# Decoding 20 of 44 float64 weights with sign and low bits taken over by ScalarE

## The chip, the cores and the metric

The kernel runs on one core of a Trainium2 chip. The metric is the device time of one execution in microseconds. The engines that matter are TensorE (PE: matrix products into PSUM), VectorE (DVE), ScalarE (ACT), GpSimd (POOL) and the DMA queues that SyncE (SP) and ScalarE issue. Each engine runs its own instructions in order and waits for the others by semaphores.

## The reference

Three stages on 8 batches of 576 tokens, cut to what matters:

```python
# attention in chunks of 64 tokens, 8 heads of 64 (q, k, v float32)
scores = 0.125 * q_c @ k_c^T;  attn = softmax(scores);  x = attn @ v_c
# first block: weights in float64
h = maximum(x @ w_in, 0);  u, v = h[..., :512], h[..., 512:]
v_n = (v - mean(v)) / sqrt(var(v) + 1e-6)
x = (u * (w_spatial @ v_n + b_spatial)) @ w_out
# second block
u = x + ((x^T @ U) @ V)^T
out = u + maximum(u @ w_ch1, 0) @ w_ch2
```

`w_in` (512x1024), `w_out` (512x512), `w_ch1` (512x2048), `w_ch2` (2048x512), `U` and `V` arrive as float64. [...]

## The kernel before

**Numbers.** Every product is made of three f16 matmuls (`mm3`, L150 to 155): both sides are split into a high half and a low half, and high x high, high x low and low x high are added in PSUM. A tile of activations so is cast by ScalarE (high half) and subtracted by VectorE or GpSimd (low half) before TensorE can use it. `x`, `xd`, `hid`, `gt`, `tr` and `ph` are such tiles.

**Weights.** The 44 weight tiles of 128 x 512 are numbered: 0 to 3 `w_u` and 4 to 7 `w_v` (the halves of `w_in`), 8 to 11 `w_o` (`w_out`), 12 to 27 `w_1` (`w_ch1`), 28 to 43 `w_2` (`w_ch2`). Each goes through a decode:

- `dec_load` (L160): a DMA brings 128 x 512 integers of 64 bits, the low word first, either into one of three buffers `st` (tag `ld4`, shared with the loads of q and k) or, for 12 of the late ones, into a part of the final weight area `wch` that is still free.
- `dec_abs` (L166): ScalarE multiplies the high words, read as float32, by 2^-111 into a buffer `dt` (L176). Late weights have two buffers `dt` (tag `o`), earlier ones three (tag `hid`, which the hidden layer uses later).
- `dec_bits` (L179): VectorE shifts `dt` left by three (L183), ORs in the top three bits of the low word (L184) and the sign bit of the high word (L187).
- `dec_parts` (L191): ScalarE casts `dt` to the high f16 half (L194) and GpSimd subtracts for the low half (L195).

**Order.** The first five attention tiles run first (`gen_first`), then weights 4 to 7 and 0 to 3 are decoded, then the spatial weights, weights 8 to 11, U and V (`gen_dec`). After that `gen_moe` for batches 0 and 1 runs, mixed with the last four early attention tiles, and the late weights 12 to 43 are handed out in the order 12, 28, 13, 29, ... (`late`, L298): whenever a piece of matmuls is done and the due time of the next weight has come, `tick` calls `next_rest`, which decodes one weight and may first copy a single element of the tile just written (`gate`, L174), so that the decode is not taken up too early. From attention tile 9 on, three streams (`gen_attn`, `gen_moe`, `gen_ch`) are merged by `Flow`, a simulated clock with costs written by hand. `gen_ch` runs the second block in 9 slices of 512 tokens; before it uses hidden block f, `want(f)` makes sure that the late weights up to 2f + 2 have been handed out. All weights are decoded by about 250 us; from then on TensorE works through attention, first block and second block without them. The instructions of this order then pass through a scheduler that simulates the engines and orders each engine's queue by it, so a change of one operation can move others on every engine.

**Names at the two places that matter.** `xd` (L419 to 421) is the attention output of the fifth tile of a pair of batches, used by `gen_moe` as `pb<-w,xd`. `rz`, `bs`, `mv` are the normalisation of `gen_moe`. `mx`, `se`, `sp` are the softmax of an attention tile (`a_softmax`, `a_norm`, L386 to 400), `ph` its f16 halves (L552, L553), which a DMA transposes to `pt` (L555); `g` and `gt` (L678 to 683) are the gated product of `gen_moe`, `hid` the hidden layer of `gen_ch` (L822, L824), `tr` the output of the first block (L746), transposed by DMA at L752.

Of the kernel before, what the change touches and what calls it, by code (L numbers as in the profile page):

```python
# [8 lines left out]
F32 = mybir.dt.float32  # L9
F16 = mybir.dt.float16  # L10
U32 = mybir.dt.uint32
I64 = mybir.dt.int64
ACTF = mybir.ActivationFunctionType
ALU = mybir.AluOpType
# [88 lines left out]
def moe_kernel(  # L103
# [12 lines left out]
    nc = tc.nc  # L116
    NT = q.shape[0]

    const = ctx.enter_context(tc.tile_pool(name="const", bufs=1))
# [36 lines left out]


    stage = {}

    def dec_load(src, name, cols, st=None, eng=nc.sync):  # L160
        if st is None:
            st = sb.tile([128, 512], I64, tag="ld4", name="st", bufs=3)
        eng.dma_start(out=st[:, 0:cols], in_=src)
        stage[name] = (st, cols)

    def dec_abs(name, g=None):  # L166
        st, cols = stage[name]
        if isinstance(name, int) and name < 12:
            t = sb.tile([128, 2, 512], F16, tag="hid", name="dt", bufs=3)
            t = t.rearrange("p a n -> p (a n)").bitcast(F32)  # L170
        else:
            t = sb.tile([128, 512], F32, tag="o", name="dt", bufs=2)
        if g is not None:
            nc.scalar.copy(out=t[0:1, 0:1], in_=g[0:1, 0:1])  # L174
        hi = st[:, 0:cols].bitcast(U32)[:, 1::2]
        nc.scalar.activation(out=t[:, 0:cols], in_=hi.bitcast(F32), func=ACTF.Copy, scale=W_SC)  # L176
        stage[name] = (st, cols, t)

    def dec_bits(name):  # L179
        st, cols, t = stage[name]  # L180
        w = st[:, 0:cols].bitcast(U32)
        tb = t[:, 0:cols].bitcast(U32)
        nc.vector.tensor_scalar(out=tb, in0=tb, scalar1=3, scalar2=None, op0=ALU.logical_shift_left)  # L183
        nc.vector.scalar_tensor_tensor(  # L184
            out=tb, in0=w[:, 0::2], scalar=29, in1=tb, op0=ALU.logical_shift_right, op1=ALU.bitwise_or
        )
        nc.vector.scalar_tensor_tensor(  # L187
            out=tb, in0=w[:, 1::2], scalar=0x80000000, in1=tb, op0=ALU.bitwise_and, op1=ALU.bitwise_or
        )
# [33 lines left out]
    def spatial_weights():  # L223
        sc = float(2 ** 14)
        for i in range(5):
            st = sb.tile([128, 512], I64, tag="ld4", name="st", bufs=3)
            f = st.bitcast(F32)[:, 0:S]
# [13 lines left out]
            yield  # L241
        st = sb.tile([128, 512], I64, tag="ld4", name="st", bufs=3)
        f = st.bitcast(F32)[:, 0:S]
# [15 lines left out]
    def gen_dec(part):  # L259
# [17 lines left out]
        def run(names, loaded=False, step=1700.0):  # L277
            n = len(names)
            for i in range(-1, n + 2):
                if i + 1 < n and not loaded:  # L280
                    ld(names[i + 1])
                if 0 <= i < n:
                    dec_abs(names[i])
                if 0 <= i - 1 < n:
                    dec_bits(names[i - 1])
                    fin(names[i - 1])
                yield "wait", step
# [12 lines left out]

    wi = wch.rearrange("p f a k n -> p (f a k n)").bitcast(I64)

# [13 lines left out]
    def next_rest(g):  # L316
        i = given[1]
        load_rest(i + 1)
        n = late[i]
        dec_abs(n, g)  # L320
        if i == 11:
            load_rest(16, nc.sync)
        elif 12 <= i < 24:
            load_rest(min(i + 4, 24))
        dec_bits(n)
        dec_parts(n)
        given[1] += 1
# [99 lines left out]
    def first_loads():  # L427

        room = []
        for tag, n, bufs in (("uT", SLICE, 2), ("uT", SLICE, 2), ("gt", S, 1), ("u32", S, 1)):  # L430
            dt, sh = (F32, [128, 4, n]) if tag == "u32" else (F16, [128, 2, 4, n])
            t = sb.tile(sh, dt, tag=tag, name="room", bufs=bufs)
            t = t.rearrange("p k n -> p (k n)") if tag == "u32" else t.rearrange("p a k n -> p (a k n)")
            t = t.bitcast(I64)
            room += [t[:, 0:512], t[:, 512:1024]]
# [557 lines left out]
```

## Time and profile before

| | us |
|---|---|
| median of three runs | 1299.94 |
| their spread | 1298.25 to 1302.38 |
| the profiled execution, its own time | 1298.71 |
| its span in the trace | 1296.9 |

| engine | busy us | share of the span |
|---|---|---|
| PE (TensorE) | 1251.6 | 97% |
| DVE (VectorE) | 507.3 | 39% |
| ACT (ScalarE) | 500.2 | 39% |
| POOL (GpSimd) | 504.5 | 39% |

The averages hide two very different stretches, so the profile is read by stretch. A line of the trace names the line of the kernel, the engine, the operation, `out<-in` by the program's names, the shapes, and the time. Times in the timeline count from the start of the span; a bracket at a row's end gives how long the engine stood idle before it and what ended that. The granted clock of TensorE averaged 0.987 of its full speed over the run.

### The profile page before, as it was taken

How to read it: one execution, taken by the hardware profiler on the slowest of the kernel's cores; microseconds unless marked ns; L12 is line 12 of the kernel's file. 1: busy time of each engine (PE TensorE's matmuls, PEld its weight loads, DVE VectorE, ACT ScalarE, POOL GpSimd, SP SyncE). 2: the span in 40 equal slices, each digit the busy share in tenths (PEclk: the TensorE clock that was granted, in tenths of full speed). 3: DMA queues.
4: the chain of work that ended last, by engine and by line, in shares of the span. 5: the costliest groups of instructions: out<-in, count | busy, mean ns of one | idle time of the engine just before them, and what ended most of it. 6: DMA issues, size and time to landing. Idle time of an engine off the chain costs nothing.

```text
span 1296.9 us, 21079 instructions
## 1 busy us (share of the span) xinstructions
PE 1251.6 (97%) x8612; PEld 708.7 (55%) x8612; DVE 507.3 (39%) x934; ACT 500.2 (39%) x1024; POOL 504.5 (39%) x630
## 2 busy tenths in 40 slices
PE   7798997999999999999999999999999999999998
PEld 4476554445665466645665466545654565444443
DVE  7885777545333633242233513241114211221211
ACT  4655556445454444433354324332123212221110
POOL 4765767637455555524365515222112211020000
PEclk8799998999999999999999999999999999999999
DMA  9445335522233322420123101200011001000000
GB/s 344 154 129 137 120 115 134 123 83 53 66 78 65 90 58 50 93 67 5 34 73 71 50 1 26 45 33 5 1 28 42 1 1 28 26 17 1 33 1 33
DMA packets 95369, 81.46 MB, mean 63 GB/s; under 512 B 69668, under 2 KB 70308, under 8 KB 95272
## 3 DMA queue, kind: packets, MB, share of 16 engines
q1 hardware_dynamic: 94120, 75.92, 21.4%
q10 hardware_dynamic: 1152, 4.19, 1.0%
q8 instruction: 67, 1.10, 0.4%
q14 instruction: 30, 0.25, 0.1%
HBM read 53.62 MB, written 9.44 MB: 49 GB/s over the span
## 4 chain that ended last, share of the span: by engine, by line
PE 80%; DVE 7%; DMA 5%; POOL 4%; ACT 2%; issue 2%; SPq 0%; DVEq 0%; POOLq 0%; ACTq 0%
PE acc L151 9%; PE phid L151 9%; PE phid L155 9%; PE phid L154 9%; PE acc L155 9%; PE acc L154 9%; PE pb L151 7%; PE pb L155 7%; PE pb L154 7%; DVE dt L184 2%; DVE dt L187 2%; DMA wch<-in_q_dram 1%; DMA tr<-tr 1%; DVE dt L183 1%; POOL wch L195 1%
## 5 line engine op out<-in xcount | busy, mean ns | idle before, releaser
L824 DVE SCALAR_TENSOR_TENSOR hid<-phid,hid 128x512 f16<-128x512 f32 x144 | 99.2, 689 | 356.4 <-ACT hid L822 356.1
L151 PE MATMUL phid<-uT,wch 128*128 128x512 f16 x576 | 218.6, 379 | 1.1 <-DVE x L786 0.6
L154 PE MATMUL phid<-uT,wch 128*128 128x512 f16 x576 | 218.6, 379 | 0.0
L155 PE MATMUL phid<-uT,wch 128*128 128x512 f16 x576 | 218.4, 379 | 0.0
L154 PE MATMUL acc<-hid,wch 128*128 128x512 f16 x576 | 218.3, 379 | 0.0
L155 PE MATMUL acc<-hid,wch 128*128 128x512 f16 x576 | 218.3, 379 | 0.0
L151 PE MATMUL acc<-hid,wch 128*128 128x512 f16 x576 | 207.9, 379 | 2.2 <-ACT hid L822 2.2
L155 PEld LDWEIGHTS <-wch 128*128 128x128 f16 x1152 | 112.8, 98 | 131.4 <-issue 0.3
L151 PEld LDWEIGHTS <-wch 128*128 128x128 f16 x1152 | 112.7, 98 | 122.4 <-issue 6.5
L154 PEld LDWEIGHTS <-wch 128*128 128x128 f16 x1152 | 112.8, 98 | 117.8 <-issue 1.7
L822 ACT ACTIVATE hid<-phid 128x512 f16<-128x512 f32 x144 | 85.4, 594 | 179.7 <-PE phid L155 179.5
L683 POOL TENSOR_TENSOR gt<-g,gt 128x288 f16<-128x288 f32 x64 | 49.3, 772 | 151.7 <-ACT gt L681 151.4
L379 POOL TENSOR_TENSOR vbd<-vf,vbd 64x512 f16<-64x512 f32 x54 | 63.9, 1183 | 91.0 <-ACT vbd L378 83.7
L749 POOL TENSOR_TENSOR tr<-x,tr 128x64 f16<-128x64 f32 x64 | 48.1, 773 | 93.1 <-issue 52.1
L366 POOL TENSOR_TENSOR qbd<-qk,qbd 64x512 f16<-64x512 f32 x54 | 62.3, 1154 | 52.1 <-ACT qbd L365 48.3
L151 PE MATMUL pb<-sp_m,vn 128*128 128x288 f16 x256 | 73.2, 286 | 2.8 <-DVE hid L824 1.5
L154 PE MATMUL pb<-gt,w 128*128 128x288 f16 x256 | 73.7, 288 | 2.1 <-POOL gt L683 2.1
L151 PE MATMUL pb<-gt,w 128*128 128x288 f16 x256 | 73.5, 288 | 1.8 <-ACT tr L746 1.7
L151 PE MATMUL pb<-xT,w 128*128 128x288 f16 x256 | 73.5, 287 | 0.7 <-ACT up L659 0.7
L155 PE MATMUL pb<-gt,w 128*128 128x288 f16 x256 | 73.6, 288 | 0.0
L154 PE MATMUL pb<-xT,w 128*128 128x288 f16 x256 | 73.5, 287 | 0.0
L155 PE MATMUL pb<-xT,w 128*128 128x288 f16 x256 | 73.5, 287 | 0.0
(177 smaller groups left out, 2224.9 us busy)
## 6 DMA issues: line engine op xcount, KB each, us to landing
st<-in_wk_dram SPq DMA_DIRECT2D x24, 512.0 KB, 4.0
out_dram<-ot SPq DMA_DIRECT2D x32, 256.0 KB, 2.0
vf<-in_v_dram SPq DMA_DIRECT2D x27, 256.0 KB, 2.7
qk<-in_q_dram SPq DMA_DIRECT2D x27, 256.0 KB, 2.7
qk<-in_k_dram SPq DMA_DIRECT2D x27, 256.0 KB, 3.0
room<-in_wk_dram SPq DMA_DIRECT2D x8, 512.0 KB, 7.2
wch<-in_wk_dram ACTq DMA_DIRECT2D x8, 512.0 KB, 4.3
wch<-in_q_dram SPq DMA_DIRECT2D x9, 256.0 KB, 6.3
```

What stands on the lines that cost most here:

```text
L151: m = nc.tensor.matmul(out=o, lhsT=wh, rhs=xh, start=start, stop=False)
L154: nc.tensor.matmul(out=o, lhsT=wh, rhs=xl, start=False, stop=False)
L155: nc.tensor.matmul(out=o, lhsT=wl, rhs=xh, start=False, stop=stop)
L183: nc.vector.tensor_scalar(out=tb, in0=tb, scalar1=3, scalar2=None, op0=ALU.logical_shift_left)
L184: nc.vector.scalar_tensor_tensor(out=tb, in0=w[:, 0::2], scalar=29, in1=tb, op0=ALU.logical_shift_right, op1=ALU.bitwise_or)
L187: nc.vector.scalar_tensor_tensor(out=tb, in0=w[:, 1::2], scalar=0x80000000, in1=tb, op0=ALU.bitwise_and, op1=ALU.bitwise_or)
L366: nc.gpsimd.tensor_tensor(out=qbd[r, 1, :, c, :], in0=qv[r], in1=qbd[r, 0, :, c, :], op=ALU.subtract)
L379: nc.gpsimd.tensor_tensor(out=vbd[r, 1, :, :, c, :], in0=vf[r], in1=vbd[r, 0, :, :, c, :], op=ALU.subtract)
L683: nc.gpsimd.tensor_tensor(out=gt[:, 1, m, c], in0=g, in1=gt[:, 0, m, c], op=ALU.subtract)
L749: nc.gpsimd.tensor_tensor(out=th[:, o0:o0 + n], in0=x2[:, m, t0:t0 + n], in1=th[:, t0:t0 + n], op=ALU.subtract)
L822: nc.scalar.activation(out=hd[:, 0, :], in_=p, func=ACTF.Relu)
L824: nc.vector.scalar_tensor_tensor(out=hd[:, 1, :], in0=p, scalar=0.0, in1=hd[:, 0, :], op0=ALU.max, op1=ALU.subtract)
```

## The change

For the weights 8 to 27 (the four of `w_o` and the sixteen of `w_1`) ScalarE gets two more operations in `dec_abs`, and VectorE keeps one of three in `dec_bits`. The first new operation reads the upper 16 bits of each low word as a number, multiplies it by 2^-13 and adds a bias of 2^-14 - 0.5 from a small constant tile, so that rounding to an integer leaves its top three bits; it writes them into the lower 16 bits of the low word. The second multiplies the high word, read as float32, by 2^-60 and writes it as f16 into the upper 16 bits of the low word, where nothing but the sign is left. The low word then holds sign and low bits in place, and one operation of VectorE shifts `dt` and ORs the word in. The weights 28 to 43 (`w_2`), 0 to 7, U and V stay as they were; since `w_1` and `w_2` alternate, every other late weight is decoded in the new way.

```diff
@@ -156,6 +157,11 @@
     stage = {}
+    low_bias = const.tile([128, 1], F32, name="low_bias")
+    nc.vector.memset(low_bias, float(2.0 ** -14 - 0.5))
+
+    def by_scalar(name):
+        return isinstance(name, int) and (8 <= name < 28)
 
@@ -174,12 +180,22 @@
         hi = st[:, 0:cols].bitcast(U32)[:, 1::2]
         nc.scalar.activation(out=t[:, 0:cols], in_=hi.bitcast(F32), func=ACTF.Copy, scale=W_SC)
+        if by_scalar(name):
+            part = st.bitcast(U16)
+            nc.scalar.activation(
+                out=part[:, 0::4], in_=part[:, 1::4], func=ACTF.Relu, scale=float(2.0 ** -13), bias=low_bias)
+            nc.scalar.activation(
+                out=part.bitcast(F16)[:, 1::4], in_=hi.bitcast(F32), func=ACTF.Copy, scale=float(2.0 ** -60))
         stage[name] = (st, cols, t)
 
     def dec_bits(name):
         st, cols, t = stage[name]
         w = st[:, 0:cols].bitcast(U32)
         tb = t[:, 0:cols].bitcast(U32)
+        if by_scalar(name):
+            nc.vector.scalar_tensor_tensor(
+                out=tb, in0=tb, scalar=3, in1=w[:, 0::2], op0=ALU.logical_shift_left, op1=ALU.bitwise_or)
+            return
         nc.vector.tensor_scalar(out=tb, in0=tb, scalar1=3, scalar2=None, op0=ALU.logical_shift_left)
```

In the changed kernel the two new operations are L185 and L187, VectorE's single one is L196, and the lines behind stand 16 further down (L176 became L182, the three old operations L199, L200 and L203, L194 became L210, L420 and L421 became L436 and L437).

**Place 1: the first use of `xd`.** On VectorE before, the stretch from the last half of `xT` to `xd`; `dt` with its numbers are the buffers of weights 8 to 10, `st` their loaded words:

```order
L414 TENSOR_TENSOR xT_199<-of_352,xT_199 128x4x128
L187 SCALAR_TENSOR_TENSOR dt_543<-st_539,dt_543 128x512
L599 TENSOR_SCALAR rz_650<-rz_650,mv_654,y_657 128x512
L183 TENSOR_SCALAR dt_547<-dt_547 128x512
L184 SCALAR_TENSOR_TENSOR dt_547<-st_541,dt_547 128x512
L636 BN_STATS bs_682<-rz_680 128x6
L187 SCALAR_TENSOR_TENSOR dt_547<-st_541,dt_547 128x512
L638 BN_AGGR mv_684<-bs_682 128x2
L183 TENSOR_SCALAR dt_556<-dt_556 128x512
L640 TENSOR_SCALAR mv_684<-mv_684 128x1
L184 SCALAR_TENSOR_TENSOR dt_556<-st_545,dt_556 128x512
L421 TENSOR_TENSOR xd_422<-of_405,xd_422 128x512
```

The same stretch of VectorE in the changed kernel, with buffer numbers two higher:

```order
L430 TENSOR_TENSOR xT_201<-of_354,xT_201 128x4x128
L196 SCALAR_TENSOR_TENSOR dt_545<-dt_545,st_541 128x512
L615 TENSOR_SCALAR rz_652<-rz_652,mv_656,y_659 128x512
L652 BN_STATS bs_684<-rz_682 128x6
L654 BN_AGGR mv_686<-bs_684 128x2
L656 TENSOR_SCALAR mv_686<-mv_686 128x1
L196 SCALAR_TENSOR_TENSOR dt_551<-dt_551,st_543 128x512
L437 TENSOR_TENSOR xd_424<-of_407,xd_424 128x512
```

Two single operations stand where six operations of the decode stood. On ScalarE before, the rows that lead to its half of `xd`:

```order
L176 ACTIVATE dt_547<-st_541 128x512
L194 CAST w8_79<-dt_543 128x512
L633 ACTIVATE rz_680<-pb_667 128x512
L603 CAST vn_608<-rz_650 128x512
L176 ACTIVATE dt_556<-st_545 128x512
L420 CAST xd_422<-of_405 128x512
```

On ScalarE in the changed kernel, the same rows (one more L185 and one more L187, those of weight 8, stand a few rows further up):

```order
L182 ACTIVATE dt_551<-st_543 128x512
L185 ACTIVATE st_543<-st_543,low_bias_93 128x512
L210 CAST w8_79<-dt_545 128x512
L649 ACTIVATE rz_682<-pb_669 128x512
L619 CAST vn_610<-rz_652 128x512
L182 ACTIVATE dt_560<-st_549 128x512
L185 ACTIVATE st_549<-st_549,low_bias_93 128x512
L187 ACTIVATE st_543<-st_543 128x512
L436 CAST xd_424<-of_407 128x512
```

Three new operations have come in among the six, and the two of weight 8 above them. On TensorE the low half of `xd` (L155 before) is now first used four matmuls later: eight products `pb<-xT,w` stand between its first two uses of the high half and it, where four stood.

**Place 2: the softmax of attention tile 9.** On VectorE before, from the maximum (`mx`) to the normalisation (`se`); `dt_2188` is a weight of `w_2`:

```order
L388 TENSOR_REDUCE mx_2221<-sp_2196 128x8
L391 TENSOR_TENSOR se_2223<-sp_2196,mx_2221 128x512
L678 SCALAR_TENSOR_TENSOR g_2267<-pb_2252,up_1691 128x288
L824 SCALAR_TENSOR_TENSOR hid_2239<-phid_2162,hid_2239 128x512
L397 TENSOR_REDUCE sp_2196<-se_2223 128x8
L183 TENSOR_SCALAR dt_2188<-dt_2188 128x512
L398 TENSOR_SCALAR sp_2196<-sp_2196 128x8
L184 SCALAR_TENSOR_TENSOR dt_2188<-wch_70,dt_2188 128x512
L399 RECIPROCAL sp_2196<-sp_2196 128x8
L187 SCALAR_TENSOR_TENSOR dt_2188<-wch_70,dt_2188 128x512
L400 TENSOR_TENSOR se_2223<-se_2223,sp_2196 128x512
```

On VectorE in the changed kernel (`dt_2246` is the next weight, one of `w_1`):

```order
L404 TENSOR_REDUCE mx_2223<-sp_2198 128x8
L407 TENSOR_TENSOR se_2225<-sp_2198,mx_2223 128x512
L840 SCALAR_TENSOR_TENSOR hid_2241<-phid_2164,hid_2241 128x512
L413 TENSOR_REDUCE sp_2198<-se_2225 128x8
L694 SCALAR_TENSOR_TENSOR g_2269<-pb_2254,up_1693 128x288
L199 TENSOR_SCALAR dt_2190<-dt_2190 128x512
L414 TENSOR_SCALAR sp_2198<-sp_2198 128x8
L196 SCALAR_TENSOR_TENSOR dt_2246<-dt_2246,st_2244 128x512
L200 SCALAR_TENSOR_TENSOR dt_2190<-wch_70,dt_2190 128x512
L415 RECIPROCAL sp_2198<-sp_2198 128x8
L203 SCALAR_TENSOR_TENSOR dt_2190<-wch_70,dt_2190 128x512
L416 TENSOR_TENSOR se_2225<-se_2225,sp_2198 128x512
```

The single operation of the next weight has come in ahead of the reciprocal. On GpSimd before, from the gated product `gt` to the low half of `ph`:

```order
L683 TENSOR_TENSOR gt_1948<-g_2184,gt_1948 128x288
L366 TENSOR_TENSOR qbd_91<-qk_1686,qbd_91 64x8x64 x2
L369 TENSOR_TENSOR kd_2226<-qk_1686,kd_2226 128x512
L195 TENSOR_TENSOR wch_70<-dt_2123,wch_70 128x512
L683 TENSOR_TENSOR gt_1948<-g_2267,gt_1948 128x288
L195 TENSOR_TENSOR wch_70<-dt_2188,wch_70 128x512
L553 TENSOR_TENSOR ph_2275<-se_2223,ph_2275 128x512
```

On GpSimd in the changed kernel:

```order
L699 TENSOR_TENSOR gt_1950<-g_2186,gt_1950 128x288
L382 TENSOR_TENSOR qbd_91<-qk_1688,qbd_91 64x8x64 x2
L385 TENSOR_TENSOR kd_2228<-qk_1688,kd_2228 128x512
L699 TENSOR_TENSOR gt_1950<-g_2269,gt_1950 128x288
L211 TENSOR_TENSOR wch_70<-dt_2190,wch_70 128x512
L211 TENSOR_TENSOR wch_70<-dt_2246,wch_70 128x512
L569 TENSOR_TENSOR ph_2277<-se_2225,ph_2277 128x512
```

`gt` now follows the splits directly, and two weights instead of one stand before `ph`. On ScalarE, a second cast (L210) and one L185 of a later weight have come in ahead of the cast of `ph`. Two pairs of L185 and L187 on words loaded straight into `wch` stand far ahead of their own weight on ScalarE: one right behind the cast of weight 0, one in the middle of the late decode.

## Rows read from the trace of the kernel before

**Rows 1.** Busy us and instructions by stretch, then TensorE's granted clock, DMA share, GB/s:

```profile
core 0: us, PE busy (x) PEld busy (x) DVE busy (x) ACT busy (x) POOL busy (x), PEclk, DMA share, GB/s
45.00:250.00 205.00, 180.03 (x1487) 114.55 (x1486) 150.39 (x253) 122.45 (x275) 137.09 (x149) 0.97 0.49 137
60.00:97.00 37.00, 33.45 (x262) 23.97 (x263) 33.56 (x68) 21.83 (x52) 23.12 (x31) 0.91 0.40 125
155.00:194.00 39.00, 36.26 (x251) 22.59 (x249) 30.22 (x48) 22.53 (x51) 23.10 (x20) 1.00 0.39 122
194.00:227.00 33.00, 25.44 (x190) 15.82 (x189) 25.81 (x36) 21.74 (x51) 24.64 (x23) 0.90 0.51 132
250.00:1296.90 1046.90, 1040.19 (x6806) 575.09 (x6804) 319.81 (x609) 353.61 (x708) 340.92 (x453) 1.00 0.16 39
```

**Rows 2.** TensorE's waits, 45 to 250 us: total us, times, longest us.

```profile
PE pb L711 <- DMA tr<-tr: 4.4, 3, 2.1
PE pb L155 <- DVE xd L421: 2.9, 1, 2.9
PE o L151 <- DMA pt<-ph: 2.8, 1, 2.8
...
PE pb L154 <- POOL gt L683: 2.1, 1, 2.1
PE pb L727 <- ACT tr L746: 1.8, 1, 1.8
PE pb L151 <- ACT tr L746: 1.7, 1, 1.7
```

**Rows 3.** VectorE's groups, 45 to 250 us: busy us, mean ns, idle before.

```profile
L187 DVE SCALAR_TENSOR_TENSOR dt<-st,dt 128x512 uint32<-128x512 uint32 x24 | 22.7, 948 | 0.4
L184 DVE SCALAR_TENSOR_TENSOR dt<-st,dt 128x512 uint32<-128x512 uint32 x24 | 22.5, 938 | 0.4
L183 DVE TENSOR_SCALAR dt<-dt 128x512 uint32<-128x512 uint32 x36 | 19.8, 550 | 13.2 <-ACT dt L176 13.0
L187 DVE SCALAR_TENSOR_TENSOR dt<-wch,dt 128x512 uint32<-128x512 uint32 x12 | 12.6, 1048 | 0.2
L184 DVE SCALAR_TENSOR_TENSOR dt<-wch,dt 128x512 uint32<-128x512 uint32 x12 | 9.5, 789 | 0.1
```

**Rows 4.** ScalarE's groups of the decode, 45 to 250 us.

```profile
L194 ACT CAST wch<-dt 128x512 f16<-128x512 f32 x32 | 19.7, 618 | 28.3 <-DVE dt L187 28.3
L176 ACT ACTIVATE dt<-st 128x512 f32<-128x512 f32 x24 | 16.0, 672 | 3.4 <-DMA st<-in_wk_dram 3.0
```

**Rows 5.** Timeline around the use of xd: start us, duration us, engine, line.

```profile
55.00 0.68 ACT L176 ACTIVATE dt<-st 128x512 f32<-128x512 f32 x1 [1.16 <-DMA st<-in_wk_dram]
...
57.67 0.57 ACT L420 CAST xd<-of 128x512 f16<-128x512 f32 x1
...
61.58 0.68 DVE L421 TENSOR_TENSOR xd<-of,xd 128x512 f16<-128x512 f32 x1
...
62.32 0.61 PE L155 MATMUL pb<-w,xd 128*128 128x512 f16 x1 [2.93 <-DVE xd L421]
```

**Rows 6.** Timeline around the softmax of attention tile 9.

```profile
192.59 0.68 DVE L388 TENSOR_REDUCE mx<-sp 128x8 f32<-128x512 f32 x1
...
197.15 1.52 DVE L184 SCALAR_TENSOR_TENSOR dt<-wch,dt 128x512 uint32<-128x512 uint32 x1
...
198.09 1.18 POOL L683 TENSOR_TENSOR gt<-g,gt 128x288 f16<-128x288 f32 x1
...
199.74 0.68 DVE L400 TENSOR_TENSOR se<-se,sp 128x512 f32<-128x512 f32 x1
...
200.45 0.62 ACT L552 CAST ph<-se 128x512 f16<-128x512 f32 x1
...
209.26 0.21 PE L151 MATMUL o<-pt,vbd 128*128 128x64 f16 x1 [2.77 <-DMA pt<-ph]
```

**Rows 7.** Timeline of ScalarE: first L176 of a decode pair, first and fifth of five.

```profile
160.42 0.65 ACT L176 ACTIVATE dt<-wch 128x512 f32<-128x512 f32 x1
...
186.77 0.68 ACT L176 ACTIVATE dt<-wch 128x512 f32<-128x512 f32 x1
```

More of the change, by code (lines that the diff above doesn't have):

```diff
@@ L11 @@
 U32 = mybir.dt.uint32
+U16 = mybir.dt.uint16
 I64 = mybir.dt.int64
```

## The prediction

> **What bounds the kernel now.** I read the profile in this order: busy time by stretch, what TensorE waits for, the costly groups of VectorE and ScalarE, then the timeline at the two places where TensorE stands longest.
>
> Busy time by stretch splits the run in two [rows 1]. From 250 us to the end TensorE is busy 1040.2 of 1046.9 us at full clock; no weight is decoded there and nothing that the diff touches stands there, so nothing is to be won or lost. All of the change lies in 45 to 250 us (two ScalarE pairs go earlier, below). There TensorE is busy 180.0 of 205 us, which leaves 25.0 us of idle time, and the granted clock is 0.97, worth about 0.03 x 205 = 6.2 us: it is 0.91 in 60 to 97 us and 0.90 in 194 to 227 us, after long waits. So 31 us is all that any relief can give. VectorE is the fullest helper there, 150.4 of 205 us (73%); GpSimd has 137.1 (67%), ScalarE 122.5 (60%). In 60 to 97 us VectorE has 33.6 of 37 us.
>
> The waits of TensorE in that stretch [rows 2] end on many things: 4.4 us on the transposing DMA of tr, 2.9 us on VectorE's low half of xd, 2.8 us on the transpose pt, 2.1 us on GpSimd's gt, and 1.8 and 1.7 us on ScalarE's tr. None ends on a weight. The decode costs time only as a crowd in front of other work.
>
> **The change part by part.**
>
> *VectorE loses two of three operations on 20 weights* (names 8 to 27). From the groups [rows 3]: L183 takes 0.550 us; the 72 runs of L184 and L187 have (22.7 + 22.5 + 12.6 + 9.5) / 72 = 0.935 us on average, the cheapest group 0.789. A weight so saves 0.55 + 0.935 = 1.49 us, 20 weights 29.7 us (26.8 with the cheapest group). The remaining operation has the old ones' form, two SBUF inputs, one of them every second word, so I keep their price. VectorE falls to 120.7 of 205 us, 59%.
>
> *ScalarE gains two activations on each of them.* The nearest rows [rows 4] are L194 (0.618 us, dense) and L176 (0.672 us, reading every second word). No row has a 16-bit output written every eighth byte, or a bias tile. I take L176's 0.672; the bounds are 0.618 and, for want of a row, twice 0.672. That is 40 x 0.672 = 26.9 us (24.7 to 53.8), and ScalarE rises to 149.3 of 205 us, 73%. So the load is not reduced, only moved: the fullest engine stays at 73%, now ScalarE, and the other two are looser.
>
> One price only a page states. The Trainium skill, "ScalarE: Activation LUTs", section "What ACT_TABLE_LOAD costs", gives about 93 ns for a per-partition pointer operand such as this bias; no row here shows one. By it ScalarE would have 20 x 0.093 = 1.9 us more, an estimate, and the sum below would hardly differ.
>
> *Order, not data, decides what is hidden.* The two new operations need only the loaded weight, not the buffer dt, and the order puts two pairs far ahead of their weight, one in the first 45 us. Their cover is ScalarE's waiting time: before L194 alone it stands 28.3 us waiting for L187 [rows 4]. Where there is no wait, what is queued behind them on ScalarE pays: the halves hid, x and tr that empty PSUM, and xd and ph, for all of which TensorE waits.
>
> *Place 1, xd.* TensorE starts the low half of xd at 62.32, after 2.93 us of waiting [rows 5]. ScalarE's half was cast at 57.67, so it was VectorE's queue that was late: its xd started at 61.58. In the new order five added activations stand before ScalarE's xd (three of L185, two of L187), 5 x 0.67 = 3.4 us, less the 1.16 us that it waited before 55.00: xd is cast at about 59.9 and ends at 60.5. VectorE has by then only its two single operations behind it and runs xd from 60.5 to 61.1. TensorE does its two first matmuls of xd later, but without the hole behind them, and four more matmuls stand in between. Gain **1.0 us** (with doubled prices xd comes at 63.3 and it is a loss of 2; without ScalarE's delay a gain of 2.9). The clock is low behind this hole; a shorter hole may keep part of it. I take 1.0 of the 3.3 us lost in 60 to 97 us (0.09 x 37) and 0.5 of the like loss in 194 to 227 us: **1.5 us** (0 to 6).
>
> *60 to 155 us.* VectorE is relieved, but TensorE's waits there are mostly the 4.4 us of tr's DMA, which nothing here touches: **0**; the gain of place 1 moves through.
>
> *155 to 194 us.* Weights go in pairs on two dt buffers: the pair starts on ScalarE go from 160.42 to 186.77 in four steps, 6.6 us each [rows 7]. Each new pair has one L183 and one two-input operation less on VectorE, 1.3 us, if ScalarE does not give it back. TensorE idles only 39 - 36.3 = 2.7 us here [rows 1], so the gain shows later, in when VectorE can turn to the softmax.
>
> *Place 2, the softmax at 192 to 209 us.* VectorE starts the maximum at 192.59, right behind a decode pair, and the normalisation at 199.74, between decode operations, one of them 1.52 us long; ScalarE casts ph at 200.45 and TensorE starts on pt at 209.26 after 2.77 us of waiting [rows 6]. New: the maximum comes earlier by its own pair (1.3) and part of the pairs before, I take 2.0 (0 to 6.5, five pairs). But one single operation of the next weight now stands inside the softmax (0.8 to 1.5 us) and a second cast and L185 stand before ph; of this I take 1.0 as what reaches pt (0.4 to 2.0). Net **1.0 us** (loss of 2.0 to gain of 6.1). The 2.1 us on gt, which GpSimd runs at 198.09 behind a weight, go too, since gt now stands ahead of that weight; but that only lengthens the wait for pt, so it counts nothing.
>
> *After 209 us.* ScalarE's tr costs 1.8 us and others less; three single operations replace nine. **0.7 us** (loss of 1.5 to gain of 2).
>
> *Sum:* 1.0 + 1.5 + 0 + 1.0 + 0.7 = 4.2 us. The profiled execution took 1298.71 us, its span 1296.9, so 1294.5; the median of the runs shown, 1299.94, lies 1.2 higher, 1295.7 from there. I say **1295 us**.
>
> **Rivals.**
>
> *Absorbed.* Place 1 gives nothing because the next hole takes it, and place 2 loses in the new interleaving what the pairs win. Then the time is 1297 to 1300. For it: helpers as a whole lose only 2.8 us of work, and waits on DMA stand between the places. Against: VectorE is the fullest queue where the longest waits start.
>
> *ScalarE becomes the bound: slower.* In 155 to 227 us ScalarE is busy 22.5 + 21.7 = 44.3 of 72 us, idle 27.7 us [rows 1], mostly in front of L194. Some nine changed weights stand there. If an added activation takes over 1.0 us, or lands in front of tr, x and hid rather than in a wait, each weight puts its pair on the path: at 1.34 us an activation, 9 x 2.7 = 24 us against 27.7 of idle in pieces; if a third shows, 8 us, less what place 1 still gives: about 1305 us. It decides from 1.0 us an activation. The Trainium skill, "ScalarE: Activation LUTs", section "Rules for kernel authors", says to give relu and multiplications to VectorE, and by that rule the swap should go this way. The rows do not bear it out for these operands: 0.94 us for an operation on VectorE against 0.67 us on ScalarE.
>
> *The decode loop was the true pace.* The chain keeps 1.3 us for each of five pairs, the clock does not fall in 194 to 227 us: 6.5 + 3.3 + 1.0 = 11 us, about 1288. Against: 2.7 us of idle in 155 to 194 us.
>
> **How the numbers follow.** About 0.3% (3.9 us) is what a measurement of this kernel can tell from no change, and the forecast lies just past it. Forecast (1292 to 1296.5) 0.40, half of a point short of the bound; absorbed 0.33; ScalarE bound 0.17; decode loop 0.10. That makes faster 0.46, same 0.37, slower 0.17. The range goes from the loop's 1288 to 1303, which leaves out the worse part of the slower rival.
>
> **What would show it.** Right: L185 and L187 at 0.6 to 0.75 us; VectorE near 121 and ScalarE near 149 us in 45 to 250 us; TensorE's low half of xd starting near 61.5; pt's wait ending a microsecond or two before 209; everything after 250 us shifted as a block. Wrong: activations over 1.0 us; new waits of TensorE on hid, x or tr; L187 of ScalarE directly ahead of them; a lower clock in 194 to 227 us.

## The result and the profile after

The changed kernel takes 1312.95 us (median of four runs, 1311.88 to 1315.22) against 1300.24 for the kernel before: 1.0100 times as long, 95% interval 1.0079 to 1.0121. The forecast was 1295 us with a range to 1303, so the change went the other way and out of the range. The profiled execution has a span of 1313.4 us.

Busy time by stretch, as in [rows 1], of the changed kernel:

```profile
core 0: us, PE busy (x) PEld busy (x) DVE busy (x) ACT busy (x) POOL busy (x), PEclk, DMA share, GB/s
45.00:250.00 205.00, 168.74 (x1376) 107.18 (x1373) 109.53 (x197) 159.15 (x297) 114.86 (x138) 0.98 0.43 127
60.00:97.00 37.00, 28.83 (x259) 20.58 (x256) 24.60 (x54) 33.00 (x60) 19.14 (x29) 1.00 0.43 131
155.00:194.00 39.00, 33.79 (x215) 20.81 (x213) 19.06 (x33) 32.54 (x59) 18.42 (x21) 1.00 0.39 135
194.00:227.00 33.00, 26.92 (x202) 16.54 (x202) 19.74 (x32) 23.74 (x48) 20.28 (x20) 0.95 0.30 81
250.00:1296.90 1046.90, 1042.19 (x6862) 577.00 (x6863) 326.67 (x619) 361.36 (x724) 352.10 (x464) 1.00 0.16 40
```

In 45 to 250 us TensorE gets through 1376 matmuls where it had 1487, and VectorE and ScalarE have changed places: VectorE went from 150.4 to 109.5 us, ScalarE from 122.5 to 159.2. From 250 us on the profile shows full clock and hardly any idle time, as before. The loss lies where the diff lies.

Where in this stretch it lies shows when TensorE's matmuls, 8612 in either trace, are counted in the order of their starts. Against the kernel before, the 500th (at 69.8 us there) starts 1.8 us earlier, the 1200th (152.7 us) 10.9 us later, the 1600th (219.3 us) 12.5 later, the 1800th (248.4 us) 17.1 later, and the last ones 16.5. The orders differ a little, so such a lag is good to some 2 us. Most of the loss has arisen by 153 us.

ScalarE's new groups up to 265 us (total busy us, mean ns of one, idle time before and its cause), to be held against [rows 4]:

```profile
L185 ACT ACTIVATE st<-st,low_bias 128x512 uint16<-128x512 uint16 x14 | 20.1, 1435 | 6.4 <-DMA st<-in_wk_dram 6.3
...
L187 ACT ACTIVATE st<-st 128x512 f16<-128x512 f32 x14 | 18.8, 1344 | 0.1
L182 ACT ACTIVATE dt<-st 128x512 f32<-128x512 f32 x24 | 16.2, 679 | 1.7 <-DMA st<-in_wk_dram 1.4
L185 ACT ACTIVATE wch<-wch,low_bias 128x512 uint16<-128x512 uint16 x6 | 8.7, 1448 | 1.6 <-DMA wch<-in_wk_dram 1.6
...
L187 ACT ACTIVATE wch<-wch 128x512 f16<-128x512 f32 x6 | 8.1, 1349 | 0.1
```

VectorE's single operation on words in `st`, in the same view; its price is near that of the old ones in [rows 3]:

```profile
L196 DVE SCALAR_TENSOR_TENSOR dt<-dt,st 128x512 uint32<-128x512 uint32 x14 | 11.5, 821 | 9.5 <-ACT st L187 3.5 <-POOL wch L211 3.0 <-ACT dt L182 2.7
```

Two things stand out on ScalarE. Each new activation takes about twice as long as the old one (1.435 and 1.344 us against L182's 0.679). And L185 has idle time before it that ends on the load of its weight, 6.4 and 1.6 us: the operation stands at the head of ScalarE's queue before its data are there. The timeline of ScalarE shows what that holds up:

```profile
105.83 1.43 ACT L185 ACTIVATE st<-st,low_bias 128x512 uint16<-128x512 uint16 x1 [2.10 <-DMA st<-in_wk_dram]
107.29 1.34 ACT L187 ACTIVATE st<-st 128x512 f16<-128x512 f32 x1
108.39 0.49 ACT L760 ACTIVATE x<-pb 128x288 f32<-128x288 f32 x1
108.78 0.39 ACT L762 ACTIVATE tr<-pb 128x288 f16<-128x288 f32 x1
```

Behind the pair stand the evictions of `x` and `tr` out of PSUM, which TensorE needs. The chain of work that ended last, followed back from the last instruction, runs through just these (start us, us): a weight's load, its pair, then the evictions of `tr` and its DMA, for which TensorE waits 2.7 us.

```profile
102.47 3.27 DMA st<-in_wk_dram
...
105.83 1.44 ACT st L185
107.29 1.34 ACT st L187
...
111.89 3.31 DMA tr<-tr
```

Of this chain in 45 to 262 us, loads of weights into `st` and `wch` hold 14.0% and 5.8% in the changed kernel and L185 another 11.6%; before, VectorE's L184, L187 and L183 led with 9.0%, 8.4% and 4.9%, and loads into `st` held 4.3%. TensorE's waits from 45 to 265 us (total us, times, longest), as in [rows 2]:

```profile
PE pb L727 <- DMA tr<-tr: 7.3, 4, 2.7
PE pb L152 <- ACT up L675: 6.3, 7, 1.7
PE pb L152 <- DVE hid L840: 5.7, 4, 2.5
PE pb L152 <- ACT rz L649: 3.0, 2, 2.5
PE pb L152 <- ACT xd L436: 2.9, 1, 2.9
PE pb L152 <- ACT tr L762: 2.7, 2, 2.4
```

The waits on VectorE's `xd` and GpSimd's `gt` no longer head the list; in their place ScalarE's `up`, `rz`, `xd` and `tr` stand, VectorE's `hid`, and more of `tr`'s DMA.

### The profile page after: what moved, and what is told of

Same layout as the page of the kernel before. It is cut to its first block, busy times and chain, and to the rows that moved or that the text cites. A ratio compares the mean times of both kernels' runs of the same rounds, so it can differ in the third digit from the quotient of the medians.

```text
span 1313.4 us, 21055 instructions
## 1 busy us (share of the span) xinstructions
PE 1254.4 (96%) x8612; PEld 708.5 (54%) x8612; DVE 477.2 (36%) x895; ACT 547.3 (42%) x1064; POOL 493.1 (38%) x630
## 4 chain that ended last, share of the span: by engine, by line
PE 80%; ACT 6%; DMA 4%; DVE 4%; POOL 3%; issue 2%; SPq 0%; DVEq 0%; ACTq 0%; POOLq 0%
PE acc L152 9%; PE phid L152 9%; PE phid L155 9%; PE phid L156 9%; PE acc L156 9%; PE acc L155 9%; PE pb L152 7%; PE pb L155 7%; PE pb L156 7%; DMA st<-in_wk_dram 2%; ACT st L185 1%; DMA wch<-in_wk_dram 1%; ACT dt L182 1%; ACT st L187 1%; DVE dt L200 1%
## 5 line engine op out<-in xcount | busy, mean ns | idle before, releaser
L155 PE MATMUL phid<-uT,wch 128*128 128x512 f16 x576 | 219.1, 380 | 0.0
L155 PE MATMUL acc<-hid,wch 128*128 128x512 f16 x576 | 218.4, 379 | 0.0
L155 PEld LDWEIGHTS <-wch 128*128 128x128 f16 x1152 | 112.9, 98 | 119.5 <-issue 3.6
L152 PE MATMUL pb<-xT,w 128*128 128x288 f16 x256 | 73.2, 286 | 6.7 <-ACT up L675 3.5
L152 PE MATMUL pb<-sp_m,vn 128*128 128x288 f16 x256 | 73.8, 288 | 5.8 <-DVE hid L840 3.0
L155 PE MATMUL pb<-gt,w 128*128 128x288 f16 x256 | 74.0, 289 | 0.3 <-POOL gt L699 0.3
L156 PE MATMUL pb<-sp_m,vn 128*128 128x288 f16 x256 | 73.9, 288 | 0.0
L155 PE MATMUL pb<-sp_m,vn 128*128 128x288 f16 x256 | 73.9, 288 | 0.0
```

The source lines that it names most:

```text
L152: m = nc.tensor.matmul(out=o, lhsT=wh, rhs=xh, start=start, stop=False)
L155: nc.tensor.matmul(out=o, lhsT=wh, rhs=xl, start=False, stop=False)
L156: nc.tensor.matmul(out=o, lhsT=wl, rhs=xh, start=False, stop=stop)
```

## The experiments

Three theories stood against each other. P: the price of the two activations made ScalarE the bound. O: their place in ScalarE's queue did, by waiting at its head. V: relief of VectorE is worth nothing here, so any load on ScalarE costs. Times are medians; each ratio is to the kernel before on the same chip, with its 95% interval.

**The price halved.**

```diff
-                out=part[:, 0::4], in_=part[:, 1::4], func=ACTF.Relu, ...
+                out=part[:, 0:1024:4], in_=part[:, 1:1024:4], func=ACTF.Relu, ...
-                out=part.bitcast(F16)[:, 1::4], in_=hi.bitcast(F32), ...
+                out=part.bitcast(F16)[:, 1:1024:4], in_=hi[:, 0:256].bitcast(F32), ...
```

> The changed kernel, but the two added activations of ScalarE treat 256 of the 512 columns, and VectorE's operation reads the words of these columns twice; signs and low bits of the other columns are left out. The two activations took 1.435 and 1.344 us in the changed kernel; with half the columns they should take about 0.7, the price that the prediction had used. Theory P (the price of the two activations made ScalarE the bound): 1294 to 1299 us, at the prediction's forecast. Theory O (they hold up ScalarE's queue by waiting at its head for a weight's load, 7.9 us of waits, whatever they cost): about 1306. Theory V (VectorE's relief is worth nothing, any load on ScalarE costs): 1301 to 1306.

Measured: 1298.53 us, ratio 0.9992 (0.9982 to 1.0003), with activations of 0.87 and 0.79 us. The loss is gone, and no gain is left: theory P's range. O's 1306 is missed, although L185 waits for loads no less than in the changed kernel (8.8 us against 7.9):

```profile
L185 ACT ACTIVATE st<-st,low_bias 128x256 uint16<-128x256 uint16 x14 | 12.1, 866 | 6.5 <-DMA st<-in_wk_dram 6.3
```

By itself this run does not isolate the price: its trace has another order of operations on every engine than the changed kernel's. The same is true of the runs with operations held in place, below.

**VectorE relieved, ScalarE not loaded** (both activations deleted, VectorE's operation an AND with the high word).

> The changed kernel without the two activations of ScalarE: VectorE still has one operation instead of three on weights 8 to 27, and signs and low bits of these weights are left out. It measures what VectorE's relief is worth by itself. Theories P and O: 1288 to 1296 us, as all that was lost came by ScalarE. Theory V: 1298 to 1302, no different from before.

Measured: 1286.47 us, ratio 0.9897 (0.9879 to 0.9915). The relief is worth 13 us, a little more than P and O had expected; theory V falls. That is about the 1288 us of the rival by which the decode loop was the true pace.

**ScalarE loaded, VectorE not relieved** (VectorE's branch for these weights switched off).

> ScalarE's two activations are added as in the changed kernel, and VectorE keeps its three operations on all weights, so nothing is relieved (the low bits are then taken from overwritten words, which leaves them out). Theory P: slower than the changed kernel by what the relief is worth, 1316 to 1325 us. Theory V: like the changed kernel, 1311 to 1315, since VectorE's relief buys nothing once ScalarE is the bound. Theory O: 1311 to 1318.

Measured: 1323.40 us, ratio 1.0181 (1.0152 to 1.0211): 10 us above the changed kernel, about the relief's worth, as P expected.

**Held in place.**

```diff
-            nc.scalar.activation(
+            tc.keep_in_program_order(nc.scalar.activation(
```

on both activations.

> The changed kernel, with the two activations held behind the first activation of their own weight on ScalarE, so that none stands far ahead of its weight; nothing else differs. Theory O: ScalarE's 7.9 us of waiting for loads at L185 go, 1303 to 1307 us. Theory P: the load of 55 us on ScalarE stays, 1309 to 1315 us, and the waits move to other lines.

Measured: 1301.82 us, ratio 1.0018 (1.0007 to 1.0030). Most of the loss goes with the price unchanged, more than O had expected and not what P had. L185's waits are gone, at the same mean duration (the orders on the other engines moved with it):

```profile
L185 ACT ACTIVATE st<-st,low_bias 128x512 uint16<-128x512 uint16 x14 | 20.0, 1432 | 0.0
```

So neither theory does alone: a lower price and another place each took most of the loss away.

**Both at once.**

> Both edits at once: ScalarE's two activations on half the columns (0.87 and 0.79 us in the run with half the columns, the other signs and low bits left out), and held behind the first activation of their own weight. The price alone came to 1298.5 us, the place in the queue alone to 1301.8, where both as changed gave 1313.0. If the two costs add (14.4 us for the price, 11 us for the place): 1286 to 1289. If they are one loss counted twice, since ScalarE then has slack enough: 1294 to 1300. If VectorE's relief is all that is left, the floor is the 1286.5 us of the run without any load on ScalarE.

Measured: 1295.27 us, ratio 0.9969 (0.9958 to 0.9981). The expectation by a sum of the two costs (1286 to 1289) is missed; the time lies in the range for one loss counted twice. With half the price the place costs 3.3 us instead of 11.1.

**The price by itself.** Operations of one form six times over, behind the last work, one operand changed at a time.

> The kernel before, with rows of six equal operations on ScalarE and VectorE on scratch tiles added behind its last work, one operand changed at a time; they lengthen the run by some 50 us and only their own durations count. If the 16-bit output at every eighth byte is what costs, every form with it takes 1.3 to 1.45 us, in place or into another tile and from a dense input too, and the same input written as 32 bits at every eighth byte or as 16 bits dense takes 0.65 to 0.75 us. If writing in place is what costs, the other tile takes 0.67. If the wide stride of the output is what costs, the 32-bit form takes 1.3 too. The form with the bias tile should take 0.09 us more than the one without, as in the changed kernel (1.435 against 1.344).

ScalarE in the stretches of one form each, in this order: 32 bits at every eighth byte in place, 16 bits at every eighth byte in place and into another tile, 16 bits at every fourth byte, 16 bits dense, 16 bits at every eighth byte from a dense input, the form of L185, and L185 with dense 16-bit and with spread 32-bit output.

```profile
L934 ACT ACTIVATE pa<-pa 128x512 f32<-128x512 f32 x6 | 4.0, 669 | 0.2
...
L934 ACT ACTIVATE pa<-pa 128x512 f16<-128x512 f32 x6 | 8.0, 1332 | 0.2
...
L934 ACT ACTIVATE pb<-pa 128x512 f16<-128x512 f32 x6 | 8.1, 1343 | 0.2
...
L934 ACT ACTIVATE pb<-pa 128x512 f16<-128x512 f32 x6 | 4.7, 782 | 0.2
...
L934 ACT ACTIVATE pb<-pa 128x512 f16<-128x512 f32 x6 | 3.9, 654 | 0.2
...
L934 ACT ACTIVATE pb<-pa 128x512 f16<-128x512 f32 x6 | 8.0, 1336 | 0.2
...
L934 ACT ACTIVATE pa<-pa,low_bias 128x512 uint16<-128x512 uint16 x6 | 8.6, 1427 | 0.2
...
L934 ACT ACTIVATE pa<-pb,low_bias 128x512 uint16<-128x512 uint16 x6 | 4.5, 745 | 0.2
...
L934 ACT ACTIVATE pa<-pb,low_bias 128x512 uint32<-128x512 uint16 x6 | 4.5, 742 | 0.2
```

What costs is a 16-bit output at every eighth byte: 1.33 to 1.34 us, into the same tile or another, from a spread or a dense input. The same place written with 32 bits takes 0.669, 16 bits at every fourth byte 0.782, dense 0.654. The form of L185 takes 1.427 - 1.336 = 0.091 us more, as expected for the bias tile; it differs in function and types too, so the bias tile alone was not timed.

**The parts of the change.** The range of weights cut to 8 to 11, and to 12 to 27.

> The change on the four weights of w_o alone (8 to 11), the sixteen of w_1 as before. It asks what place 1, the use of xd, gives by itself; the prediction had 1.0 us of gain and the clock behind it. With the activations at 1.4 us ScalarE's half of xd comes late: 1300 to 1304 us. If the relief of VectorE there still counts: 1297 to 1299.

> The change on the sixteen weights of w_1 alone (12 to 27). If the loss comes from the load on ScalarE weight by weight, it is 16/20 of the 13 us: 1309 to 1312 us. If a good part of it comes from place 1: 1303 to 1308.

Measured: 1302.16 us (1.0016, 1.0005 to 1.0027) and 1307.75 us (1.0057, 1.0040 to 1.0075). The four weights of `w_o` alone are a small loss, in the range for a late `xd`, for which TensorE waits 2.94 us. But the loss is not made there: the 625th matmul (83.1 us before) still starts 0.5 us earlier than before, and the 1000th (119.8 us) 4.5 us later. The sixteen later weights carry most, in the range that was given for a good part of the loss coming from place 1.

**Packed words.** The probe shows a cheaper form: whole 32-bit words (0.742 us), here packed, and the sign at every fourth byte (0.782).

```diff
-                out=part[:, 0::4], in_=part[:, 1::4], func=ACTF.Relu, ...
+                out=st.bitcast(U32)[:, 0:512], in_=part[:, 1::4], func=ACTF.Relu, ...
-                out=part.bitcast(F16)[:, 1::4], in_=hi.bitcast(F32), func=ACTF.Copy, ...
+                out=part.bitcast(F16)[:, 1:1024:2], in_=t, func=ACTF.Copy, ...
-                ... in1=w[:, 0::2], ...
+                ... in1=w[:, 0:512], ...
```

> The same result as the changed kernel with dense words: on weights 8 to 27 ScalarE writes the three low bits as whole 32-bit words, packed into the first half of the loaded buffer (0.742 us by the probe's 32-bit row), then the sign, read from dt, as f16 into every second half-word of these (0.775 us by the probe's row for 16 bits at every fourth byte); VectorE's single operation reads packed words. Both must follow the first activation of their weight, so nothing is hoisted. Price 1.52 us a weight instead of 2.78. Theory P and the place in the queue together: like the run with half the columns held in place, 1293 to 1297 us, faster than before by 0.2 to 0.5%. If VectorE's relief had been worth something only because ScalarE was also left alone: 1298 to 1302.

> The packed form on the sixteen weights of w_1 alone (12 to 27); w_o as before. If place 1, the use of xd, still loses by ScalarE's late cast there (the changed form on w_o alone came to 1302.2, 2.3 us slower than before): 1291 to 1295 us, faster than with w_o. If VectorE's relief at place 1 is worth its price now: 1295 to 1299, slower than with w_o.

Measured: 1286.94 us (0.9904, 0.9889 to 0.9919) and 1291.49 us (0.9942, 0.9930 to 0.9955); in both the sign was lost in the product with 2^-60, so signs are left out there. The first is better than either expectation. The second is a mixed miss: in the level that was given for the first case, but 4.6 us slower than with `w_o`, so relief on the weights of `w_o` does pay once it is cheap.

> The packed form on weights 8 to 27 once more, with the sign written at a scale of 1 instead of 2^-60, which keeps it (in the run before, that product came out as plain zero, so the signs of these weights were left out there). Each engine's instructions are the same ones in the same order, so the time should be the same: 1285 to 1289 us against about 1299.5, whether the price or the place in the queue is the cause. If the lost signs had made that run quicker by themselves: 1293 to 1297.

Measured: 1287.00 us, ratio 0.9900 (0.9885 to 0.9914). This version beats both kernels, by 12.5 us and by 26, with nothing left out.

> The packed form on all weights from 8 to 43, 36 instead of 20. VectorE is relieved of a further 16 x 1.49 = 24 us, ScalarE loaded with a further 16 x 1.55 = 25 us, to about 178 of 205 us. If what counts is the sum over both engines, not much changes: 1284 to 1290 us. If ScalarE becomes the bound as it did in the changed kernel (159 busy of 205 us there): 1293 to 1303.

Measured: 1287.21 us, ratio 0.9899 (0.9879 to 0.9920). No further gain and no loss, though ScalarE is busy 170.4 of the 205 us there, more than in the changed kernel:

```profile
45.00:250.00 205.00, 190.55 (x1565) 119.71 (x1563) 99.40 (x186) 170.41 (x354) 129.57 (x153) 0.98 0.49 141
```

A busy ScalarE alone is not the bound.

> The packed form on weights 8 to 27 with the sign's activation issued three times over, so that ScalarE has 0.77 + 3 x 0.78 = 3.1 us a weight, about as in the changed kernel (2.78), with VectorE's operation and the dependences as in the packed form. If ScalarE's price is the cause, the gain goes: 1299 to 1306 us, like the changed form held in place (1301.8 at 2.78 us a weight). If the packed form gains by its order or by the packed words that VectorE reads, and the price hardly matters: 1287 to 1294.

Measured: 1293.42 us, ratio 0.9954 (0.9940 to 0.9969). This is within the second expectation, at its upper end: half of the gain is left under twice the load.

**The price alone, in an equal order.**

```diff
-                out=st.bitcast(U32)[:, 0:512], in_=part[:, 1::4], func=ACTF.Relu, ...
+                out=part[:, 3::4], in_=part[:, 1::4], func=ACTF.Relu, ...
-                out=part.bitcast(F16)[:, 1:1024:2], in_=t, func=ACTF.Copy, scale=1.0)
+                out=part.bitcast(F16)[:, 3::4], in_=t, func=ACTF.Copy, scale=1.0)
-                ... in1=w[:, 0:512], ...
+                ... in1=w[:, 1::2], ...
```

> The packed form with nothing changed but where ScalarE's two activations write: 16 bits at every eighth byte, as in the changed kernel, over the high words. Each engine has the same instructions in the same order as in the packed form (the low bits are spoiled and so left out). Price 2.77 us a weight instead of 1.55, 24 us more on ScalarE in all. If the price is the larger part of the loss: 1298 to 1306 us, which is 11 to 19 above the packed form, near the changed form held in place (1301.8). If it was rather the order that the changed form got: 1289 to 1294, as the run with three signs, which had more load yet (1293.4) but an order made with that load in it.

Measured: 1305.71 us, ratio 1.0048 (1.0030 to 1.0066). Groups of ScalarE on `st` in 45 to 250 us, first of the packed form, then of this one:

```profile
L187 ACT ACTIVATE st<-dt 128x512 f16<-128x512 f32 x14 | 11.0, 782 | 0.1
...
L185 ACT ACTIVATE st<-st,low_bias 128x512 uint32<-128x512 uint16 x14 | 10.8, 770 | 0.3
```

```profile
L185 ACT ACTIVATE st<-st,low_bias 128x512 uint16<-128x512 uint16 x14 | 20.2, 1441 | 0.3
...
L187 ACT ACTIVATE st<-dt 128x512 f16<-128x512 f32 x14 | 18.8, 1341 | 0.1
```

The two traces have the same instructions in the same order on TensorE, VectorE, ScalarE and GpSimd, next to no wait at L185 in either (0.3 us), and 1305.71 - 1287.00 = 18.7 us between them. VectorE's single operation is no rival: on words in `st` it took 0.76 us in the spread form and 0.92 in the packed one. Some 4 us of the difference come by the granted clock, 0.97 against 0.99 in these 205 us, an estimate from two profiles. So price alone, in one order, is the larger part of the 26 us that lie between the packed and the changed kernel.

It isn't all. The engines' line of the profile's page, for this run and for the one with three signs:

```profile
PE 1253.5 (96%) x8612; PEld 708.5 (54%) x8612; DVE 476.0 (37%) x895; ACT 549.3 (42%) x1064; POOL 498.6 (38%) x630
```

```profile
PE 1246.9 (97%) x8612; PEld 705.5 (55%) x8612; DVE 478.8 (37%) x895; ACT 549.9 (43%) x1104; POOL 496.8 (38%) x630
```

ScalarE has about 550 us and VectorE 476 and 479, yet 12.3 us lie between the two (1305.7 and 1293.4). What differs is how the load came into the order. Three signs are three operations that the scheduler places; a doubled duration leaves its order as it was, as the equal order of the packed and the spread form shows. The pieces are shorter, too, and in the trace of three signs other work stands between them (signs of one weight at 90.57, 91.53 and 92.48 us, each time a cast of `gt` between). Whether the other order or the shorter pieces gain the 12 us, no run shows.

## Why the prediction was wrong

**What bounds the kernel: right.** Nothing was lost after 250 us, and the relief of VectorE is real. Over the whole run VectorE's busy time fell by 507.3 - 477.2 = 30.1 us, forecast 29.7, and taken alone that is worth 13 us. The prediction had put the decode loop as the pace at 1288 us and a chance of 0.10; without a load on ScalarE (1286.5), or with a cheap one (1287.0), that is where the kernel goes, and largely for that rival's reason. By the count of matmuls the run without the load gains 11 us between the 1200th and the 1600th (153 to 219 us), with TensorE busy 39.0 of 39 us in 155 to 194 and a granted clock of 1.00 in 194 to 227; the rival had 6.5 + 3.3 there.

**The price of the two activations: the step that failed.** The prediction took 0.672 us from L176, with twice that as the far bound, 26.9 us in all. It was 20.1 + 18.8 + 8.7 + 8.1 = 55.7 us, just past the bound of 53.8. L176 was nearest by operation and input, but it writes 32 bits, dense. The prediction named the difference, a 16-bit output at every eighth byte, and then took the price of the row that lacks it. That its far bound, 1.344 us, is almost the price was luck: twice was taken for want of a row. So its comparison of 0.94 us on VectorE with 0.67 on ScalarE did not hold: two activations at 2.78 us replaced two operations at about 1.49.

What the price alone does, the packed and the spread form show: 18.7 us in one order. The rival that ScalarE becomes the bound decided from 1.0 us an activation, and the runs lie on both sides of that as it says: at 0.87 and 0.79 us the time equals that of before, at 1.44 and 1.34 it is 13 us longer. No run lies near 1.0, and held in place 1.43 us cost only 2.5. The rival had a chance of 0.17, too little for a cost with no row of its own. Its 8 us were too few, and it looked for them in 155 to 227 us, where the lag grows from 10.9 to only 12.5 us, though there the relief's 11 us are lost as well.

**Place 1: the bound came true, not the value taken.** With doubled prices the cast of `xd` was put at 63.3 and the loss at 2 us. The timeline of the changed kernel, against [rows 5]:

```profile
62.94 0.67 ACT L436 CAST xd<-of 128x512 f16<-128x512 f32 x1
...
63.66 0.39 PE L152 MATMUL pb<-w,xd 128*128 128x512 f16 x1 [2.95 <-ACT xd L436]
...
63.83 0.68 DVE L437 TENSOR_TENSOR xd<-of,xd 128x512 f16<-128x512 f32 x1
...
65.08 0.38 PE L156 MATMUL pb<-w,xd 128*128 128x512 f16 x1
```

TensorE waits 2.95 us as before, now for ScalarE's half, and the low half is first used at 65.08 instead of 62.32, with four more matmuls done by then: a loss of some 2 us, as the bound said. The clock makes it good at once, 1.00 in 61.5 to 67.5 us instead of 0.50: at the 500th matmul the changed kernel is 1.8 us ahead. In the packed form the cast starts at 59.38, where the prediction had it at 59.9:

```profile
59.38 0.59 ACT L436 CAST xd<-of 128x512 f16<-128x512 f32 x1
...
60.02 0.39 PE L152 MATMUL pb<-w,xd 128*128 128x512 f16 x1 [0.83 <-ACT xd L436]
```

**The clock: right by luck, and drowned.** In 60 to 97 us the granted clock rose from 0.91 to 1.00, the upper level (2.4 GHz). The prediction hoped for that from a shorter hole, but the hole was no shorter (2.95 us), and in the run on `w_o` alone a hole of 2.94 us was followed by 3 us at 0.50, the lower of its two levels (1.2 GHz). In the changed kernel the lower level came later instead: 0.97 in 97 to 155 us, where it had been 1.00, and 0.95 in 194 to 227. Busy TensorE fell from 33.45 to 28.83 us in 60 to 97, partly since matmuls at full clock are shorter (0.38 us here, 0.61 in [rows 5]), partly since it stood idle.

**Place 2: late on arrival.** The maximum starts 12.3 us later than in [rows 6] and TensorE starts on `pt` 12.8 later, so the softmax itself adds only half a microsecond to a delay that is already there, where a gain of 1.0 was forecast:

```profile
204.91 0.67 DVE L404 TENSOR_REDUCE mx<-sp 128x8 f32<-128x512 f32 x1
...
214.11 0.68 DVE L416 TENSOR_TENSOR se<-se,sp 128x512 f32<-128x512 f32 x1
...
222.10 0.19 PE L152 MATMUL o<-pt,vbd 128*128 128x64 f16 x1 [0.95 <-DMA pt<-ph]
```

The term for the time after 209 us, 0.7 of gain, had the wrong sign: from the 1600th matmul to the 1800th (219 to 248 us before) the lag grows from 12.5 to 17.1 us.

**60 to 155 us: a zero that was not one.** The prediction put 0 here, since TensorE waits there mostly for `tr`'s DMA, and took ScalarE's waits as cover for what moves ahead in its queue. Most of the loss was made here. The later part of the stretch, before and in the changed kernel:

```profile
97.00:155.00 58.00, 51.82 (x484) 33.63 (x483) 37.15 (x68) 33.64 (x79) 38.67 (x50) 1.00 0.46 125
```

```profile
97.00:155.00 58.00, 48.48 (x440) 32.09 (x438) 28.09 (x53) 37.44 (x77) 32.81 (x45) 0.97 0.40 108
```

An operation whose data come late was seen to wait at the head of ScalarE's queue with evictions behind it. That is not all of it. At the 1200th matmul (153 us) the changed kernel lags by 10.9 us, held in place by 6.6, with half the columns by 5.7 and with both by 7.0, while the packed form is 1.3 us ahead. What made the loss in this stretch when the price was low and L185 did not wait is not shown.

**Had the price been right?** No run has that price in the order of the changed kernel. The nearest, half the columns at 0.87 and 0.79 us in an order of its own, comes to 1298.5 us, in the range of the rival "absorbed", not of the forecast. The sum of small gains was too hopeful for that order, and too small for a better one (1287.0).

**What stays open.** Kernels with the same load on ScalarE and VectorE differ by up to 12 us: 1298.5, 1295.3 and 1287.0 at about 526 us of ScalarE, 1305.7 and 1293.4 at about 550. About equal load and unequal order are shown; which of the moved operations make these microseconds was not taken apart.

## What to carry to other kernels

Price a new operation by the row that shares its output pattern, not its name, and where no row does, give the far bound a real chance or time the form by itself first. Operations that depend only on a load can be drawn ahead in an in-order queue; ask what stands behind them when the load is late, and try tying them to the work they belong to (here 11 of the 13 us). When an engine is loaded by something that the scheduler does not see, its order is made for another kernel: about the same load cost 12 us less where it came as operations that were placed one by one.

## What the runs showed of the hardware

A 16-bit write at every eighth byte costs ScalarE twice a dense one, 1.336 against 0.654 us for 128 x 512, though a 32-bit write at the same places takes 0.669. VectorE pays as well, 0.734 us against 0.427; its three outputs from one input, spread 16 bits, spread 32 bits and dense 16 bits:

```profile
L959 DVE TENSOR_SCALAR pb<-pa 128x512 f16<-128x512 f32 x6 | 4.4, 734 | 55.3 <-ACT pa L934 55.1
L962 DVE TENSOR_SCALAR pb<-pa 128x512 f32<-128x512 f32 x6 | 2.6, 428 | 0.2
L965 DVE TENSOR_SCALAR pb<-pa 128x512 f16<-128x512 f32 x6 | 2.6, 427 | 0.2
```

The Trainium skill, "ScalarE: Activation LUTs", section "What ACT_TABLE_LOAD costs", gives one element a cycle for every function, for fp32 and bf16 alike; the spread 16-bit output does not follow that, and the measurement decides. Its 93 ns for a pointer operand agree with the 0.091 us that the form with the bias tile takes more here, though function and types differ between the two forms as well.
